# The denominator's epsilon by a one-row matmul, and the order of decode and division in the attention steps

## The chip, the cores and the metric

The kernel runs on one core of a Trainium2 chip. The metric is the device time of one execution in microseconds (us). It stood at 959.82 us, the median of three runs (958.62 to 960.18).

## The reference

A linear attention with random features, then two feed-forward layers; all inputs and outputs are fp32.

```python
q_s, k_s = (q * scale, k * scale)          # q, k, v: batch 4, 8 heads, 576 rows, head_dim 64
def phi(x):                                # omega: 128 features x 64
    proj = np.einsum('bhsd,md->bhsm', x, omega)
    sq = np.sum(x * x, axis=-1, keepdims=True) / 2.0
    h = proj - sq
    h = h - np.max(h, axis=-1, keepdims=True)
    return np.exp(h) / np.sqrt(m)
kv = np.einsum('bhsm,bhsd->bhmd', k_p, v)
z = np.sum(k_p, axis=2)
num = np.einsum('bhsm,bhmd->bhsd', q_p, kv)
den = np.einsum('bhsm,bhm->bhs', q_p, z)[..., None] + 1e-06
attn = num / den
x = attn as 2304 rows x 512
h = x @ w_in;  g = max(h, 0) + alpha * min(h, 0);  x = g @ w_out      # 512 -> 2048 -> 512
a = x @ w_a;  b = x @ w_b;  out = (a * b) @ w_out2                    # 512 -> 1536 -> 512
```

## The kernel before

**The work.** The attention is cut into 40 pieces: eight units `u` (a batch and a group of four heads) by five row tiles `t` (four of 128 rows, a last one of 64). It runs as a software pipeline of steps `s`. In one step `a_proj` (L724) projects a piece of k and an earlier piece of q into two banks `pp`; `a_max` (L738) takes row maxima `nm` from them on VectorE; `a_exp` (L747) makes `ph` by up to eight `Exp` on ScalarE; `a_kv` (L762) adds a piece to the states `kv` (the ones column in `v` also gives the sum z); `a_num` (L793) multiplies the transposed features `phT` of a q piece by the states `kvp`, into one bank `nd` of four slots of 65 columns, of which the last is the denominator; `a_t` (L779) transposes the next q piece on TensorE (`tp`) and copies it to `phT`; `a_x` (L815) transposes the divided rows `xn` (`xp`) into `xT`. `ev` (L834) gives the step of each: k and q at their step, `kv` one step after k, `t` two, `num` three and `x` four steps after q.

**The division** is in `a_num`: a `tensor_scalar` adds `EPS * M` to the four denominators read from the bank, a `reciprocal` works on the result in SBUF, and a `tensor_tensor` multiplies the 4 x 64 numerators by it. The scale of `EPS * M` is that of features left without their 1/sqrt(M).

**The steps.** The first 15 stand alone. From then on a step stands inside a step of the first feed-forward layer (class `Mlp`): `a_front` (L515) makes a 256-column `h` of 12 fp32r matmuls, ScalarE takes its two ReLU halves (`u`, `h`), VectorE joins them (`h`), ScalarE and VectorE split the result in a high and a low part (`gh`, `gl`), and in the middle of that `attn_next` (L943) puts one attention step; `a_back` (L551) makes `y`. `a_x` is put off to `A.flush()` between two such steps. `pp`, `nd`, `tp`, `xp` and `h` take turns in five PSUM banks.

**Decode.** The weights come as 64-bit words. The `Decoder` (L212) turns each piece of 128 x 512 into two fp32r parts: `bits` (L255) does four instructions on VectorE (`z`, `a`, `c`, `c`), `piece` (L283) then copies `a` to the high part `w` on ScalarE (L289) and forms the low part in two instructions, most often on GpSimd (L290, L291). It is a generator, and `D_.go(n)` (L414) takes n strides of it; three strides issue the four VectorE instructions, the fourth `w` and the low part.

**What sets the order.** Every engine works its instructions in the order in which the code issues them (`tc.manual_schedule()`); nothing reorders them. `attn_2` (L882) therefore says how decode stands against states, division and transposes:

```python
        D_.go(3)
        if s in ev["kv"]:
            a_kv(*ev["kv"][s])
        if s in ev["num"]:
            a_num(*ev["num"][s])
        D_.go()
        if s in ev["t"]:
            a_t(*ev["t"][s])
```

After the attention, the rest of the first layer and the second layer (Winograd-like products `W`, `E`, `B` and the output product `o`) follow on TensorE.

Of the kernel before, what the change touches and what calls it, by code (L numbers as in the profile page):

```python
# [9 lines left out]
F32 = mybir.dt.float32  # L10
# [3 lines left out]
ALU = mybir.AluOpType  # L14
# [4 lines left out]
P = 128  # L19
NB, NH, S, D = 4, 8, 576, 64  # L20
M = 128
# [9 lines left out]
EPS = 1e-6  # L31
# [34 lines left out]
def tile_kernel(ctx: ExitStack, tc: tile.TileContext, qT, kT, v1, omT, wbits, alpha, out):  # L66
    nc = tc.nc
# [70 lines left out]
    def pick(*ways):  # L138

        def worst(w):  # L140
            return max(load[e] + w.get(e, 0.0) for e in load)

        i = min(range(len(ways)), key=lambda i: worst(ways[i]))
        for e, x in ways[i].items():
            load[e] += x
        return i
# [63 lines left out]
    tensor, vector = Watch(nc.tensor, pe_cost), Watch(nc.vector, dve_cost)  # L210
# [239 lines left out]
    D_ = Decoder()  # L450
# [218 lines left out]
    def rpool(st, **kw):  # L669
        return st.enter_context(tc.tile_pool(side=RIGHT, **kw))  # L670

    ac = rpool(st_a, name="ac", bufs=1)
# [20 lines left out]
    def load_k(u):  # L693
        t = ld.tile([P, 2 * S], F32, tag="k", name=f"k{u}")
        if u == 0:
            nc.scalar.dma_start(out=t[:, 0:256], in_=kT[u][:, 0:256])
            nc.sync.dma_start(out=t[:, 256:], in_=kT[u][:, 256:])
        else:
            if u == 1:
                after_dve(t)  # L700
            nc.sync.dma_start(out=t, in_=kT[u])
        t_k[u] = t
# [15 lines left out]
    def slots_of(t):  # L718
        return 4 if t < 4 else 2

    def bank(name, pool=None):
        return (pool or psp[0]).tile([P, 512], F32, tag="ps", name=name)
# [39 lines left out]
    def a_kv(u, t):  # L762
        if t == 0:
            kvt[u] = pskv.tile([P, 4, D + 1], F32, tag="kv", name=f"kv{u}")
        kv = kvt[u]
        ph = phik.pop((u, t))
        for h in range(4):

            for r in (slice(0, M // 2), slice(M // 2, M)):
                tensor.matmul(kv[r, h, :], lhsT=ph[:, h if t < 4 else h % 2, r],  # L770
                                 rhs=t_v[u][:, t * VC + h * (D + 1):t * VC + (h + 1) * (D + 1)],
                                 start=(t == 0 and h == 0), stop=(t == 4 and h == 3))
        if t == 4:

            load["act"] += 0.4
            nc.scalar.activation(kvp[u % 3], kv, AF.Copy)
            kvt.pop(u)

    def a_t(u, t):  # L779

        ns = slots_of(t)
        ph = phiq.pop((u, t))
        pp = bank(f"tp{u}_{t}").rearrange("p (o m) -> p o m", m=P)
        for h in range(ns):
            tensor.transpose(pp[:, h, :], ph[:, h, :], ident)
        d = pq.tile([P, 4, P], F32, tag="phT", name=f"phT{u}_{t}", bufs=2)
        if pick({"act": 0.1 + 0.13 * ns}, {"dve": 0.1 + 0.15 * ns}):
            vector.tensor_copy(d[:, :ns], pp[:, :ns])
        else:
            nc.scalar.activation(d[:, :ns], pp[:, :ns], AF.Copy)  # L790
        phT[u, t] = d

    def a_num(u, t):  # L793


        ns = slots_of(t)
        d = phT.pop((u, t))
        kv = kvp[u % 3]
        nd = bank(f"nd{u}_{t}")[:, :4 * (D + 1)].rearrange("p (o e) -> p o e", e=D + 1)
        for h in range(ns):  # L800
            for a in range(2):
                r = slice(a * 64, a * 64 + 64)

                tensor.matmul(nd[r, h, :], lhsT=d[:, h, r], rhs=kv[:, h if t < 4 else 2 * a + h, :],
                                 start=True, stop=True)
        load["dve"] += 0.35 + 0.13 * ns
        rc = sm.tile([P, 4], F32, tag="rc", name=f"rc{u}_{t}")
        vector.tensor_scalar(out=rc[:, :ns], in0=nd[:, :ns, D], scalar1=EPS * M, scalar2=None, op0=ALU.add)
        vector.reciprocal(out=rc[:, :ns], in_=rc[:, :ns])
        xn = pq.tile([P, 4, D], F32, tag="xn", name=f"xn{u}_{t}", bufs=2)  # L810
        vector.tensor_tensor(out=xn[:, :ns], in0=nd[:, :ns, 0:D],
                                in1=rc[:, :ns].unsqueeze(2).to_broadcast([P, ns, D]), op=ALU.mult)
        xns[u, t] = xn
# [67 lines left out]

    def attn_2(s):  # L882

        D_.go(3)
        if s in ev["kv"]:
            a_kv(*ev["kv"][s])
        if s in ev["num"]:
            a_num(*ev["num"][s])
        D_.go()
        if s in ev["t"]:  # L890
            a_t(*ev["t"][s])

    def attn_3(s):
        if s in ev["x"]:
            a_x(*ev["x"][s])
# [4 lines left out]
    nc.sync.dma_start(out=om_raw, in_=omT)  # L900
    load_k(0)
    warm = ac.tile([P, P], F32, name="warm")
    vector.memset(warm, 0.0)
    make_identity(nc, ident)
    vector.tensor_scalar(out=om, in0=om_raw.rearrange("p (k n) -> p k n", n=64), scalar1=scale, scalar2=None, op0=ALU.mult)
# [8 lines left out]
    if True:  # L914
        w_ = bank("warm")
        for i in range(WARM):
            tensor.matmul(w_[:, 0:P], lhsT=warm, rhs=warm, start=True, stop=True)
        for s in range(SPLIT_AT):
            D_.step(DEC0[0] if s < 3 else DEC0[1] if s < Q_LAG else DEC0[2])
            passed(1.3 if s < Q_LAG else 4.5)  # L920
            pj = attn_1(s)
            nm = a_max(*pj)
            loads(s)

            for k in range(KT):
                if s > x_step[k // 2, (CI - 1) // P]:
                    A.split(0, 0, CI, k)
            a_exp(*pj, nm)
            if s == 3:
                D_.start(0)  # L930
            if s == Q_LAG + 1:
                nc.sync.dma_start(out=nalpha, in_=alpha)
            attn_2(s)
            attn_3(s)
        vector.tensor_scalar(out=nalpha, in0=nalpha, scalar1=-1.0, scalar2=None, op0=ALU.mult)
    st_z.close()

    with st_m:
# [4 lines left out]
        def attn_next(high=None, low=None):  # L943
            s = nxt_s[0]
            nxt_s[0] += 1
            D_.step(DEC1)
            pj = attn_1(s)
            if high:
                high()
            if pj:  # L950
                nm = a_max(*pj)
            loads(s)
            if low:
                low()
            if pj:
                a_exp(*pj, nm)
            attn_2(s)
            A.after.append(lambda: attn_3(s))
# [378 lines left out]
```

## Time and profile before

| what | value |
|---|---|
| median of the runs | 959.82 us |
| the profiled execution, own time | 958.08 us |
| its span | 956.3 us |
| TensorE (PE) busy | 937.0 us, 98% |
| TensorE weight loads (PEld) busy | 843.5 us, 88% |
| VectorE (DVE) busy | 673.4 us, 70% |
| ScalarE (ACT) busy | 515.5 us, 54% |
| GpSimd (POOL) busy | 165.0 us, 17% |
| granted TensorE clock, mean | 0.999 of full |

The profile is one execution. The shares are means over stages with different limits: attention steps fill some 235 us at the start, so the table tells little of them, and the prediction goes by stretches. A matmul's end is modelled, so a busy TensorE may still be waiting for a part of a modelled end; what is sure of a matmul is its start. An fp32 matmul shows as two records, a transpose as one.

### The profile page before, as it was taken

What the parts mean: (1) busy time and instruction counts of PE and PEld (TensorE: products, weight loads), DVE (VectorE), ACT (ScalarE), POOL (GpSimd) and SP (SyncE); (2) the same over time, 40 slices, a digit from 0 to 9 for tenths busy, and PEclk for the clock granted to TensorE, in tenths of its full rate; (3) what the DMA queues carried; (4) which work ended last, traced back from release to release, by engine and by line L of the source; (5) the groups of instructions that cost most, each with busy time, mean ns of one, the idle gap of its engine ahead of it and who ended that gap; (6) DMA issues with size and microseconds to landing.
All of it is one profiled execution on the core that took longest, in us unless ns stands there. A gap on an engine that the chain in (4) does not pass through costs nothing.

```text
span 956.3 us, 16788 instructions
## 1 busy us (share of the span) xinstructions
PE 937.0 (98%) x6486; PEld 843.5 (88%) x6486; DVE 673.4 (70%) x1343; ACT 515.5 (54%) x1237; POOL 165.0 (17%) x135
## 2 busy tenths in 40 slices
PE   7889999999999999999999999999999999999998
PEld 6778899989988878889888899999999999989897
DVE  5898855555488887768766978977686975673733
ACT  6877766655455545345544546564464554554531
POOL 3686700000056541001000000000001011110101
PEclk9999999999999999999999999999999999999999
DMA  8544422000123332304536756259828288523323
GB/s 302 171 163 148 136 77 77 26 23 24 46 88 113 108 111 88 132 22 144 202 118 219 294 213 220 77 185 372 312 86 226 58 251 273 142 34 100 43 57 66
DMA packets 47696, 132.65 MB, mean 139 GB/s; under 512 B 4352, under 2 KB 10752, under 8 KB 47616
## 3 DMA queue, kind: packets, MB, share of 16 engines
q1 hardware_dynamic: 42720, 122.79, 36.9%
q0 software_dynamic: 4752, 8.65, 6.0%
q8 instruction: 51, 0.84, 0.4%
q14 instruction: 29, 0.24, 0.1%
q10 hardware_dynamic: 144, 0.13, 0.0%
HBM read 87.52 MB, written 44.04 MB: 138 GB/s over the span
## 4 chain that ended last, share of the span: by engine, by line
PE 81%; DVE 9%; ACT 6%; issue 2%; DMA 2%; SPq 0%; DVEq 0%; ACTq 0%
PE y L188 17%; PE h L188 16%; PE o L188 15%; PE W L188 15%; PE E L188 7%; PE B L188 4%; ACT ph L757 3%; DVE a L188 2%; DVE z L188 1%; DVE c L188 1%; PE tp L188 1%; DVE h L188 1%; PE nd L188 1%; PE kv L188 1%; DMA store<-t_None 1%
## 5 line engine op out<-in xcount | busy, mean ns | idle before, releaser
L188 PE MATMUL h<-xh,w 128*128 128x256 f32 (+1 forms) x768 | 204.5, 340 | 0.2 <-DVE yo L188 0.2
L188 PE MATMUL y<-gh,w 128*128 128x256 f32 (+1 forms) x768 | 202.0, 338 | 0.9 <-ACT gh L539 0.9
L188 PEld LDWEIGHTS y<-gh,w 128*128 128x128 f32 x768 | 134.5, 189 | 16.5 <-ACT gh L539 1.6
L188 PEld LDWEIGHTS h<-xh,w 128*128 128x128 f32 x768 | 135.0, 189 | 15.8 <-DVE yo L188 0.4
L188 PE MATMUL o<-w,gh 128*128 128x512 f32 x432 | 133.2, 389 | 0.0
L188 PE MATMUL y<-gl,w 128*128 128x512 f32 (+1 forms) x384 | 129.3, 337 | 0.4 <-DVE gl L188 0.2
L188 PE MATMUL h<-xl,w 128*128 128x512 f32 (+1 forms) x384 | 129.0, 336 | 0.2 <-DVE xl L500 0.2
L188 DVE SCALAR_TENSOR_TENSOR h<-u,nalpha,h 128x256 f32<-128x256 f32 (+1 forms) x96 | 59.5, 620 | 72.9 <-ACT h L527 71.9
L526 ACT ACTIVATE u<-h 128x256 f32<-128x256 f32 (+1 forms) x96 | 47.2, 492 | 98.0 <-PE h L188 94.8
L1236 POOL DMA_DIRECT2D out<-op x30 | 26.3, 877 | 422.2 <-ACT op L163 344.2
L188 PEld LDWEIGHTS o<-w,gh 128*128 128x128 f32 x432 | 81.0, 188 | 16.5
L539 ACT ACTIVATE gh<-h 128x256 fp32r<-128x256 f32 (+1 forms) x96 | 47.1, 491 | 78.7 <-DVE h L188 78.5
L188 PE MATMUL o<-w,gl 128*128 128x512 f32 x216 | 84.2, 390 | 0.0
L290 POOL TENSOR_TENSOR a<-a,w 128x512 f32<-128x512 f32 x32 | 47.2, 1474 | 212.2 <-ACT w L289 207.2
L188 PEld LDWEIGHTS y<-gl,w 128*128 128x128 f32 x384 | 72.7, 189 | 8.7 <-DVE gl L188 1.3
L188 PEld LDWEIGHTS h<-xl,w 128*128 128x128 f32 x384 | 72.7, 189 | 7.9 <-DVE xl L500 0.5
L188 DVE TENSOR_TENSOR gl<-h,gh 128x256 fp32r<-128x256 f32 (+1 forms) x96 | 53.1, 553 | 23.6 <-ACT gh L539 22.5
L163 ACT ACTIVATE u<-W 128x384 f32<-128x384 f32 x72 | 35.0, 491 | 45.7 <-PE W L188 44.6
L188 DVE TENSOR_SCALAR z<-z 128x512 uint32<-128x512 uint32 x68 | 39.8, 585 | 24.6 <-ACT z L249 24.5
L188 DVE SCALAR_TENSOR_TENSOR a<-raw,z 128x512 uint32<-128x512 uint32 x68 | 54.0, 794 | 2.3
L163 ACT ACTIVATE op<-o 128x512 f32<-128x512 f32 x51 | 30.4, 596 | 44.4 <-PE o L188 36.6
L188 DVE SCALAR_TENSOR_TENSOR c<-raw,c 128x512 f32<-128x512 uint32 x68 | 48.5, 714 | 2.3
(492 smaller groups left out, 1987.1 us busy)
## 6 DMA issues: line engine op xcount, KB each, us to landing
raw<-in_w SPq DMA_DIRECT2D x68, 512.0 KB, 4.2
w<-store SPq DMA_DIRECT2D x39, 512.0 KB, 6.6
store<-t_None SPq DMA_DIRECT2D x34, 512.0 KB, 3.8
st<-ypart SPq DMA_DIRECT2D x14, 768.0 KB, 8.0
out<-op POOLq DMA_DIRECT2D x30, 256.0 KB, 5.2
v<-in_v SPq DMA_DIRECT2D x8, 650.0 KB, 6.0
q<-in_qT SPq DMA_DIRECT2D x8, 576.0 KB, 3.8
yp<-ypart SPq DMA_DIRECT2D x4, 1024.0 KB, 7.5
```

What stands on the lines that cost most here:

```text
L163: nc.scalar.activation(out, in_, AF.Copy)
L188: return call(*a, **k)
L290: eng.tensor_tensor(out=a, in0=a, in1=hi.bitcast(F32), op=ALU.subtract)
L526: nc.scalar.activation(u_, hp, AF.Relu, scale=-1.0)
L539: nc.scalar.activation(gh, hp, AF.Copy)
L757: nc.scalar.activation(ph[:, 2 * pr + j], pair[j][:, o + pr], AF.Exp, bias=nm[:, j, o + pr:o + pr + 1])
L1236: nc.gpsimd.dma_start(out=dst, in_=op, accum_op=ALU.add)
```

## The change

It touches three places. In `a_num`, the matmuls of a bank now form one accumulation group, which a further matmul of one row closes: 128 ones times four (or two) values `EPS * M`, added to the denominator columns in the bank. The `tensor_scalar` is gone and the `reciprocal` reads the bank. In `attn_2`, the three decode strides come after `a_kv` and `a_num`, and the fourth after `a_t`. At the start GpSimd fills the row.

```diff
@@ a_num
                 tensor.matmul(nd[r, h, :], lhsT=d[:, h, r], rhs=kv[:, h if t < 4 else 2 * a + h, :],
-                                 start=True, stop=True)
+                                 start=(h == 0), stop=False, skip_group_check=True)
         load["dve"] += 0.35 + 0.13 * ns
+        tensor.matmul(nd[:, :ns, D], lhsT=row[:, :P], rhs=row[:, P:P + ns], start=False, stop=True, skip_group_check=True)
         rc = sm.tile([P, 4], F32, tag="rc", name=f"rc{u}_{t}")
-        vector.tensor_scalar(out=rc[:, :ns], in0=nd[:, :ns, D], scalar1=EPS * M, scalar2=None, op0=ALU.add)
-        vector.reciprocal(out=rc[:, :ns], in_=rc[:, :ns])
+        vector.reciprocal(out=rc[:, :ns], in_=nd[:, :ns, D])
         xn = pq.tile([P, 4, D], F32, tag="xn", name=f"xn{u}_{t}", bufs=2)
@@ attn_2
-        D_.go(3)
         if s in ev["kv"]:
             a_kv(*ev["kv"][s])
         if s in ev["num"]:
             a_num(*ev["num"][s])
-        D_.go()
+        D_.go(3)
         if s in ev["t"]:
             a_t(*ev["t"][s])
+        D_.go()
@@ before the first step
     warm = ac.tile([P, P], F32, name="warm")
+    row = ac.tile([1, P + 4], F32, name="row")
+    nc.gpsimd.memset(row[:, :P], 1.0)
+    nc.gpsimd.memset(row[:, P:], EPS * M)
```

The order of instructions shows what moves. The three places below are of one attention step inside the first layer, the one that projects unit 4's first piece (`pp(4, 0)`); names are those of the text above, with a number behind them.

VectorE, before: from `gl` of this step to the joining `h` of the next.

```order
L188 TENSOR_TENSOR gl_256_1_1402<-h_256_1_1384,gh_256_1_1401 128x256
L188 TENSOR_SCALAR z_1344<-z_1344 128x512
L188 SCALAR_TENSOR_TENSOR a_1432<-raw_1199,z_1344 128x512
L188 TENSOR_SCALAR c_1433<-a_1432 128x512
L188 SCALAR_TENSOR_TENSOR c_1433<-raw_1199,c_1433 128x512
L188 TENSOR_SCALAR rc_1_1458<-nd_1_1449 128x4
L188 RECIPROCAL rc_1_1458<-rc_1_1458 128x4
L188 TENSOR_TENSOR xn_1_1461<-nd_1_1449,rc_1_1458 128x256
L188 SCALAR_TENSOR_TENSOR h_256_2_1477<-u_256_2_1490,nalpha,h_256_2_1477 128x256
```

The same place, now.

```order
L188 TENSOR_TENSOR gl_256_1_1405<-h_256_1_1387,gh_256_1_1404 128x256
L188 RECIPROCAL rc_1_1452<-nd_1_1442 128x4
L188 TENSOR_TENSOR xn_1_1454<-nd_1_1442,rc_1_1452 128x256
L188 TENSOR_SCALAR z_1369<-z_1369 128x512
L188 SCALAR_TENSOR_TENSOR a_1458<-raw_1220,z_1369 128x512
L188 TENSOR_SCALAR c_1459<-a_1458 128x512
L188 SCALAR_TENSOR_TENSOR c_1459<-raw_1220,c_1459 128x512
L188 SCALAR_TENSOR_TENSOR h_256_2_1480<-u_256_2_1493,nalpha,h_256_2_1480 128x256
```

The division has moved ahead of the four decode instructions and is one instruction shorter.

ScalarE, before: after the step's `Exp`, from the copy of the states to the next ReLU half.

```order
L776 ACTIVATE kvp_168<-kv_1019 128x260
L289 ACTIVATE w_88<-a_1432 128x512
L790 ACTIVATE phT_0_1471<-tp_0_1466 128x512
L831 ACTIVATE xT<-xp_0_1473 128x2x128
L526 ACTIVATE u_256_2_1490<-h_256_2_1477 128x256
```

The same place, now.

```order
L776 ACTIVATE kvp_168<-kv_1012 128x260
L790 ACTIVATE phT_0_1471<-tp_0_1466 128x512
L289 ACTIVATE w_88<-a_1458 128x512
L831 ACTIVATE xT<-xp_0_1476 128x2x128
L526 ACTIVATE u_256_2_1493<-h_256_2_1480 128x256
```

The weight copy `w` and the copy of the transposed features `phT` have changed places.

TensorE, before: from the states to the next `h`.

```order
L188 MATMUL kv_1019<-v_674,ph_4_1331 64x65 x8
L188 MATMUL nd_1_1449<-kvp_170,phT_1_1379 64x65 x8
L188 MATMUL tp_0_1466<-ident,ph_0_1190 128x128 x4
L188 MATMUL xp_0_1473<-ident,xn_0_1369 128x128 x2
L188 MATMUL h_256_2_1477<-xh_256_0_961,w_82 128x256
```

The same place, now.

```order
L188 MATMUL kv_1012<-v_677,ph_4_1334 64x65 x8
L188 MATMUL nd_1_1442<-kvp_170,phT_1_1379 64x65 x8
L188 MATMUL nd_1_1442<-row 128x4
L188 MATMUL tp_0_1466<-ident,ph_0_1193 128x128 x4
L188 MATMUL xp_0_1476<-ident,xn_0_1362 128x128 x2
L188 MATMUL h_256_2_1480<-xh_256_0_964,w_82 128x256
```

One matmul stands between the numerators and the transposes, in each of the 40 pieces; TensorE's order is otherwise the same, and so is that of the DMA queue.

## Rows read from the trace of the kernel before

**Rows 1.** Busy time by stretch; columns: stretch, length, PE, PEld, DVE, ACT, POOL, clock, DMA.
```profile
24.00:85.00 61.00, 54.31 (x730) 47.03 (x732) 54.44 (x130) 47.45 (x151) 40.34 (x29) 1.00 0.47 150
85.00:122.00 37.00, 36.23 (x451) 33.85 (x448) 29.77 (x70) 26.59 (x81) 27.53 (x19) 1.00 0.46 151
122.00:240.00 118.00, 116.67 (x1417) 108.36 (x1416) 65.81 (x193) 71.85 (x233) 0.00 (x0) 1.00 0.14 46
240.00:956.00 716.00, 710.73 (x3633) 638.12 (x3631) 509.87 (x919) 354.96 (x725) 89.17 (x77) 1.00 0.46 147
```

**Rows 2.** PE's waits from 24 to 85 us: sum, times, longest.
```profile
PE nd L188 <- ACT phT L790: 2.7, 4, 1.2
PE xp L188 <- ACT ph L757: 2.0, 3, 1.0
```

**Rows 3.** PE's waits from 85 to 240 us, all of them.
```profile
PE xp L188 <- ACT ph L757: 1.0, 2, 0.5
PE xp L188 <- DVE gl L188: 0.8, 3, 0.3
PE xp L188 <- DVE xn L188: 0.2, 1, 0.2
```

**Rows 4.** Timeline of DVE in a step: start, duration (us), instruction.
```profile
54.49 0.41 DVE L188 TENSOR_SCALAR z<-z 128x512 uint32<-128x512 uint32 x1
...
56.74 0.15 DVE L188 TENSOR_SCALAR rc<-nd 128x4 f32<-128x4 f32 x1
56.92 0.18 DVE L188 RECIPROCAL rc<-rc 128x4 f32<-128x4 f32 x1
57.14 0.42 DVE L188 TENSOR_TENSOR xn<-nd,rc 128x256 f32<-128x256 f32 x1
57.60 0.49 DVE L188 SCALAR_TENSOR_TENSOR h<-u,nalpha,h 128x256 f32<-128x256 f32 x1
```

**Rows 5.** Timeline around a wait of `nd`, ACT and PE.
```profile
23.76 0.75 ACT L289 ACTIVATE w<-a 128x512 fp32r<-128x512 f32 x1
...
24.28 0.71 ACT L790 ACTIVATE phT<-tp 128x512 f32<-128x512 f32 x1
...
25.05 0.69 PE L188 MATMUL nd<-kvp,phT 128*64 128x65 f32 x16 [1.18 <-ACT phT L790]
```

**Rows 6.** Timeline of PE, one step; a cut window shows a group's later records alone.
```profile
172.51 0.61 PE L188 MATMUL pp(7, 1)_False<-xT,q 64*128 64x128 f32 x8
...
172.74 0.39 PE L188 MATMUL pp(7, 1)_False<-xT,q 64*128 64x128 f32 x4
173.06 0.28 PE L188 MATMUL kv<-v,ph 128*64 128x65 f32 x2
...
173.16 0.58 PE L188 MATMUL kv<-v,ph 128*64 128x65 f32 x14
173.57 0.23 PE L188 MATMUL nd<-kvp,phT 128*64 128x65 f32 x2
...
173.75 0.46 PE L188 MATMUL nd<-kvp,phT 128*64 128x65 f32 x10
174.14 0.33 PE L188 MATMUL tp<-ident,ph 128*128 128x128 f32 x1
...
174.31 0.49 PE L188 MATMUL tp<-ident,ph 128*128 128x128 f32 x3
174.55 0.36 PE L188 MATMUL y<-gh,w 128*128 128x256 f32 x1
```

**Rows 7.** Records of `nd` by stretch (PE first; 16 are a piece, 8 a short one).
```profile
85.00:122.00 37.00, 3.60 (x88) 3.08 (x88) 3.33 (x12) 1.00 0.46 151
122.00:240.00 118.00, 13.24 (x312) 10.93 (x312) 11.96 (x44) 1.00 0.14 46
```

**Rows 8.** Timeline of PE and of DVE, the step with least time between `nd` and decode.
```profile
27.86 0.64 PE L188 MATMUL nd<-kvp,phT 128*64 128x65 f32 x16
...
28.72 0.42 DVE L188 TENSOR_SCALAR z<-z 128x512 uint32<-128x512 uint32 x1
```

## The prediction

> **What bounds the kernel now.** I read the busy time by stretch first, since the whole page mixes stages. Until about 85 us no engine is full: from 24 to 85 us TensorE is idle for 61.00 - 54.31 = 6.69 us and VectorE for 6.6 us [rows 1]. From 85 us on TensorE is the bound: it is idle for 0.77 us of 37 and for 1.33 us of 118 while the attention lasts, and for 5.3 us of the 716 after it, at full clock throughout [rows 1]. So time that VectorE saves can shorten the kernel only before 85 us, and time that TensorE gets to do lengthens it wherever TensorE is the bound.
>
> The waits of TensorE say what it waits for. Before 85 us the largest are for `phT`, 2.7 us in four waits, and for banks or data behind the `Exp`, 2.0 us in three [rows 2]. After it only `xp` waits, six times and 2.0 us in all [rows 3]; it waits for `xn` just once, for 0.2 us. So the divided rows are not what is late, and bringing the division ahead of decode is worth little by itself.
>
> **The change part by part.**
>
> *The add that goes.* On VectorE the `tensor_scalar` takes 0.15 us, and from its start to that of the reciprocal it is 56.92 - 56.74 = 0.18 us [rows 4]; that is what each piece saves there. How long a reciprocal takes that reads the bank is in no row. The nearest are the removed `tensor_scalar` from the same bank, 0.15 us, and the reciprocal from SBUF, 0.18 us [rows 4]; I take 0.18 us for it, and a saving of 0.18 us.
>
> *Decode behind the division.* In 15 of the 40 pieces the four decode instructions stood ahead of the division; from the `z` at 54.49 to the `tensor_scalar` at 56.74 that is 2.25 us [rows 4]. They now come later by the division, and the next `h` or `nm` on VectorE comes after both as before: the sum on the engine is the same, less the 0.18 us. Behind the wait that is added stand the four decode instructions, then the next maxima: the reciprocal must now find the bank complete at once. In the tightest step the numerators end at 27.86 + 0.64 = 28.50 us, and decode began at 28.72 [rows 8]; what the new matmul adds to the bank's completion, some 0.3 us, nearly fits. I cost the move at nothing, with 0.1 us in each of the two or three early steps if the cover is gone. The raw words are loaded in the same order.
>
> *`phT` ahead of `w`.* On ScalarE `w` at 23.76 keeps `phT` to 24.28, so 0.52 us; `nd` waits for it until 25.05, after 1.18 us of idle time [rows 5]. Where `phT` is on the path, that is won: I count it in two of the four waits [rows 2], less what the new matmul then adds to the same path of `nd`, `tp` and the next projection. `w` and the low part on GpSimd come 0.5 us later; no wait of TensorE for a weight stands in either list [rows 2, 3], so that is free.
>
> *The new matmul.* It has weights of one row by 128 columns, between `nd` of form 128\*64 and `tp` of 128\*128, so it is a form of its own. What a change of form costs is seen in one step [rows 6]. Pairs of `pp` records follow each other by (172.74 - 172.51) / 2 = 0.115 us, and pairs of `kv` records by (173.57 - 173.16) / 7 = 0.059 us. From `pp` to `kv` the last pair takes 173.06 - 172.74 - 0.115 = 0.205 us, 0.09 more than a pair, and the first `kv` pair 0.10 us, 0.04 more: 0.13 us for the change. From `nd` to `tp` it is 174.14 - 173.75 = 0.39 us for five pairs, 0.10 more than 5 x 0.059; then 0.17 us for the first transpose, against (174.55 - 174.31) / 2 = 0.12: 0.15 us. So one more change of form costs 0.13 to 0.15 us. Its two records cost as little as a `kv` pair each, 0.059 us, or as much as a `pp` pair, 0.115 us: together 0.25 to 0.38 us per piece. With no change of form at all it would be 0.12 us, and 0.06 us if the records ran side by side as those of a pair do; nothing lower, since TensorE's queue is in order and full. I take 0.30 us: the weights have the 128 columns of `pp`, but hardly any columns stream. I keep 0.06 and 0.38 us for the range.
>
> The Trainium skill (TensorEngine Tiling (Array Packing), Key Properties) has it that a change of tiling mode drains TensorE. The 0.09 and 0.10 us at the ends of `pp` and `nd` agree. The same skill (TensorE: Matmul & The Clock Gate, LDWEIGHTS) says that a load goes by its columns and not by its rows, about 107 ns for 128, so one row would save nothing; no row here has such a load alone. By that page the two loads would be an estimated 0.21 us, and the piece 0.35 us.
>
> *The sum.* After 85 us lie 88 + 312 = 400 records of `nd` [rows 7], which are 22 pieces of 16 and 6 short ones of 8: 28 pieces, 28 x 0.30 = 8.4 us on the bound engine. The six waits of `xp` hide part: each hides at most its own length or 0.30 us, so about 0.6 + 0.8 + 0.2 = 1.6 us [rows 3]. That leaves +6.8 us. Before 85 us, the path goes by VectorE and ScalarE. I count two times 0.52 us for `phT` less 0.30 us for the matmul on that path, 0.4 us; eight of the twelve pieces, in which VectorE is the path, by 0.18 us, 1.4 us; and take off two pieces in which the path has already moved to TensorE, 0.6 us, and 0.2 us for decode's lost cover. That is -1.0 us. The two fills of the row on GpSimd come before the identity is needed, some 20 us later, and cost nothing. Sum: +5.8 us. The profiled execution took 958.08 us, 1.74 us under the median; it would take 963.9 us, and I forecast 959.82 + 5.8 = **965.6 us** for the median.
>
> **The rivals.**
>
> *The matmul is cheap, and nothing changes.* If the one-row form costs no change, a piece costs 0.12 us, and 28 pieces 3.4 us, of which the waits hide 6 x 0.12 = 0.7 us; with 2.0 us won before 85 us the sum is +0.7 us: 960.5 us. For it speaks that the matmul writes four columns alone; against it, that both changes of form in the step cost time [rows 6]. The Trainium skill (TensorEngine Tiling (Array Packing), Instruction Overhead) supports the cheap case: about 60 cycles for any small matmul, by which two records are an estimated 0.05 us and 28 pieces 1.4 us; the transposes and `kv` pairs here are too long to show it.
>
> *VectorE's relief is worth all of its length, and the kernel is faster.* In the 15 pieces with decode VectorE is nearly full, so each 0.18 us may be won until 122 us, 2.7 us, and `phT` adds 2 x 0.52 = 1.0 us: 3.7 us, which the 6.69 us of idle time before 85 us [rows 1] can hold. With the matmul at 0.06 us (28 x 0.06 - 0.4 = +1.3 us) the sum is -2.4 us: 957.4 us. It decides where a piece's matmul costs less than about 0.08 us, since 22 unhidden pieces then give back no more than 1.8 us of the 3.7. Against it: from 85 to 122 us VectorE is busy for 29.77 of 37 us, so not the bound [rows 1].
>
> *The full price, and VectorE held.* At 0.38 us a piece, 28 pieces are 10.6 us, less 1.9 us hidden, with nothing won before 85 us because the reciprocal waits with decode and maxima behind it: +8.7 us, 968.5 us. This is the upper part of my range. That the change does not do what it says, a reciprocal from the bank as long as the 0.33 us of both instructions before, would take 1.4 us from the gain, and is inside the range too.
>
> **How the numbers follow.** A difference within 0.2%, 1.9 us, is about what a measurement of this kernel cannot tell from no change. The forecast, slower by 2 to 10 us, with the full price at its upper end, gets 0.70; the cheap matmul without a gain 0.15; the faster case 0.15. So faster 0.15, same 0.15, slower 0.70. The range goes from 958.0 us, inside the cheap case, to 969.5 us, a little over the full price; what is left out is most of the faster case and a rest above, under 0.2 together.
>
> **What would show it.** Right: in steps after 85 us the distance from `nd`'s first record to `tp`'s grows from 0.57 us by 0.25 to 0.38 us, with the new records in between; TensorE has no new idle time there; the step at the end of the attention comes some 6 us later than before; the 716 us after it keep their length. On VectorE the reciprocal follows `gl` without idle time, at 0.15 to 0.25 us; at 85 us the kernel stands 0 to 3 us ahead. Wrong: if that distance grows by less than 0.13 us, the price of the form failed; if it grows by 0.3 us and the kernel still isn't slower, TensorE was not the bound where I say so; if VectorE waits ahead of the reciprocal, the cover of the move was gone.

## The result, and the profile after

The changed kernel takes **967.98 us**, the median of five runs (966.15 to 968.65); before stood at 959.82 us in five runs beside them. The ratio is 1.0082, with an interval of 1.0072 to 1.0093: 8 us slower. Forecast were 965.6 us in a range of 958.0 to 969.5.

The profiled execution took 968.65 us, with a span of 966.9 us; it is the slowest of the five, while the profiled one of before was among the fastest of its kernel, so that the two traces differ by 10.57 us, 2.4 more than the medians. Part of this spread goes with the clock, in both kernels alike: after takes 966.15 us at a mean granted clock of 1.000 and 968.65 at 0.995 and 0.996, and of 61 executions of before that ran beside the experiments the 13 at 1.000 have a median of 958.19 us and the 24 at 0.997 or less one of 959.88.

The busy time of after by stretch, with the columns of [rows 1]:

```profile
24.00:85.00 61.00, 55.68 (x748) 49.38 (x746) 53.24 (x115) 46.40 (x150) 38.65 (x27) 0.97 0.47 150
85.00:122.00 37.00, 36.44 (x461) 33.87 (x460) 30.69 (x67) 27.35 (x83) 26.86 (x20) 1.00 0.45 153
122.00:240.00 118.00, 117.80 (x1416) 110.14 (x1415) 59.20 (x161) 69.29 (x224) 2.28 (x2) 1.00 0.13 42
240.00:956.00 716.00, 712.62 (x3669) 641.46 (x3668) 511.61 (x927) 358.59 (x735) 88.34 (x76) 1.00 0.46 146
```

From 85 us on TensorE was nearly full before and is fuller now: 117.80 of 118 us, where it was 116.67. New in this table is the 0.97 in the clock's column of the first row: in the changed kernel the clock was not full all the time ahead of 85 us; in [rows 1] it is 1.00 there.

TensorE's waits in after, from 24 to 85 us (two rows) and, behind the dots, from 85 to 240 us (one row, all there is); they answer to [rows 2, 3]:

```profile
PE xp L188 <- ACT ph L757: 2.3, 3, 1.5
PE nd L188 <- ACT phT L790: 1.8, 3, 0.7
...
PE xp L188 <- ACT ph L757: 0.8, 2, 0.6
```

`nd` waits less for `phT` (1.8 us, was 2.7), `xp` a little more before 85 us, and of the 2.0 us of waits behind 85 us 0.8 are left.

One step of TensorE in after, the same as in [rows 6]:

```profile
177.67 0.64 PE L188 MATMUL nd<-kvp,phT 128*64 128x65 f32 x16
178.23 0.38 PE L188 MATMUL nd<-row 1*128 1x4 f32 x2
178.54 0.66 PE L188 MATMUL tp<-ident,ph 128*128 128x128 f32 x4
```

The new matmul is two records. From the first `nd` to the first `tp` it is 178.54 - 177.67 = 0.87 us, where [rows 6] have 174.14 - 173.57 = 0.57; from the 7th piece on, every piece with a `tp` behind it takes 0.30 or 0.31 us more than before. In VectorE's timeline of the same step the reciprocal reads the bank and takes 0.17 us, with no idle time ahead of it. It waits for the bank in one piece alone, the first (last row):

```profile
178.51 0.42 DVE L188 TENSOR_TENSOR gl<-h,gh 128x256 fp32r<-128x256 f32 x1
178.84 0.17 DVE L188 RECIPROCAL rc<-nd 128x4 f32<-128x4 f32 x1
179.05 0.43 DVE L188 TENSOR_TENSOR xn<-nd,rc 128x256 f32<-128x256 f32 x1
...
26.22 0.18 DVE L188 RECIPROCAL rc<-nd 128x4 f32<-128x4 f32 x1 [0.29 <-PE nd L188]
```

Where the time of the two profiled executions parts is read from the starts of three pieces' numerators, the 1st, the 13th and the last, on TensorE. (The start of the 1st says little by itself: over the fourteen traces of this study it lies anywhere from 24.1 to 27.6 us.) Before (the 1st is in [rows 5]):

```profile
85.30 0.64 PE L188 MATMUL nd<-kvp,phT 128*64 128x65 f32 x16
...
234.15 0.45 PE L188 MATMUL nd<-kvp,phT 128*64 128x65 f32 x8
```

After:

```profile
25.18 0.69 PE L188 MATMUL nd<-kvp,phT 128*64 128x65 f32 x16 [0.67 <-ACT phT L790]
...
86.81 0.64 PE L188 MATMUL nd<-kvp,phT 128*64 128x65 f32 x16
...
241.56 0.45 PE L188 MATMUL nd<-kvp,phT 128*64 128x65 f32 x8
```

| stretch | before, us | after, us | difference |
|---|---|---|---|
| to the 1st piece | 25.05 | 25.18 | +0.1 |
| 1st to 13th | 60.25 | 61.63 | +1.4 |
| 13th to 40th | 148.85 | 154.75 | +5.9 |
| 40th to the end of the span | 722.15 | 725.34 | +3.2 |

The last row is not the change's: `nd` is done by then. It comes from one place near 745 us, where ScalarE waits for a store to land (first row) and TensorE behind it (second row); the last two rows show the 4 us that follow, with the columns of [rows 1].

```profile
745.41 0.42 ACT L163 ACTIVATE t<-a 128x256 fp32r<-128x256 f32 x1 [6.58 <-DMA store<-t_None]
...
746.26 0.44 PE L188 MATMUL W<-xh11A,w 128*128 128x384 f32 x1 [2.23 <-ACT u L163]
...
747.00:749.00 2.00, 2.00 (x9) 2.00 (x8) 1.93 (x5) 1.07 (x3) 0.00 (x0) 0.53 0.01 4
749.00:751.00 2.00, 2.00 (x9) 2.00 (x8) 2.00 (x5) 0.00 (x0) 0.00 (x0) 0.62 0.86 238
```

TensorE waits 2.23 us for `W`, 0.7 in before, and then runs 4 us at a clock of 0.53 and 0.62. In the profiled execution of the first experiment, which has the new matmul too, the same stretch takes 722.2 us (962.7 - 240.53), as in before; of the twelve experiments' traces eleven have 721.4 to 723.3 us there, with a new matmul or without, and one 725.7. So the differences that belong to the change are +1.4 us, where a gain of 1.0 was forecast, and +5.9, where 6.8 were.

### The profile page after: what moved, and what is told of

Its sections match the earlier page's. It is cut to its first block, busy times and chain, and to the rows that moved or that the text cites. A ratio compares the mean times of both kernels' runs of the same rounds, so it can differ in the third digit from the quotient of the medians.

```text
span 966.9 us, 16931 instructions
## 1 busy us (share of the span) xinstructions
PE 948.3 (98%) x6566; PEld 856.3 (89%) x6566; DVE 669.6 (69%) x1303; ACT 515.7 (53%) x1237; POOL 165.2 (17%) x137
## 4 chain that ended last, share of the span: by engine, by line
PE 82%; DVE 8%; ACT 5%; issue 2%; DMA 2%; SPq 0%; DVEq 0%; ACTq 0%
PE y L188 16%; PE h L188 16%; PE W L188 15%; PE o L188 15%; PE E L188 7%; PE B L188 4%; ACT ph L757 2%; PE nd L188 2%; DVE a L188 2%; DVE z L188 2%; PE tp L188 1%; PE kv L188 1%; DVE c L188 1%; DMA store<-t_None 1%; DVE h L188 1%
```

## The experiments

Two questions stood: is the new matmul the whole loss, and by what, its change of form or its records; and what did the new order do before 85 us? At first the theory was the prediction's price of the form; the rivals were the records alone, and the order. Ratios are to before, run on the same chip beside the kernels that are compared with it; its median was 959.92 us in 19 runs, 959.24 in 29 and 959.35 in 13. Where a kernel ran once, no ratio is given.

### The two halves of the change apart

The first kernel keeps the new matmul and the reciprocal from the bank, and puts `attn_2` back:

```diff
+        D_.go(3)
         if s in ev["kv"]:
...
             a_num(*ev["num"][s])
-        D_.go(3)
+        D_.go()
         if s in ev["t"]:
             a_t(*ev["t"][s])
-        D_.go()
```

> The changed kernel with decode put back ahead of states and division; the one-row matmul and the reciprocal from the bank stay. Theory A (the matmul's price on a full TensorE): nd to tp stays 0.31 us longer, and the time stays 6 to 8 us over the kernel before, 966 to 968 us. Theory B (the moved order: weight copies, GpSimd and VectorE late, TensorE idle and then at the lower clock): at most half of the loss is left, 963 us or less.

Measured: 965.81 us in four runs (964.08 to 968.13), ratio 1.0070 (1.0046 to 1.0094). From the 1st to the 13th piece it takes 85.47 - 24.94 = 60.53 us, from there to the last 240.53 - 85.47 = 155.06, 6.2 us more than before.

The second is the kernel before with the new `attn_2` alone:

```diff
-        D_.go(3)
         if s in ev["kv"]:
...
             a_num(*ev["num"][s])
-        D_.go()
+        D_.go(3)
         if s in ev["t"]:
             a_t(*ev["t"][s])
+        D_.go()
```

> The kernel before with the new order alone; add and reciprocal stay two VectorE instructions. Theory A: within 1.5 us of the kernel before, 958.5 to 961.5 us, since decode's sum on VectorE is unchanged. Theory B: at least half of the loss, 963 us or more, with TensorE idle near 49 us and a stretch at the lower clock behind it.

Measured: 961.11 us in ten runs (958.67 to 962.58), ratio 1.0017 (1.0006 to 1.0028). From the 1st to the 13th piece 87.66 - 25.39 = 62.27 us, 2.0 more than before; from there to the last 148.68, 0.2 less. The time is in the range of theory A; the trace, below, has the idle TensorE and the lower clock of theory B.

So the matmul costs 0.70% or 6.7 us, by the trace nearly all of it behind 85 us; the new order costs 0.17% or 1.6 us, by the trace ahead of 85 us. Together that is 8.3 us, and the whole change cost 8.2. That they add up so well is partly luck: by the intervals the matmul costs 4.4 to 9.0 us and the order 0.6 to 2.7. The order, of which a gain was forecast, is a loss.

### What the matmul costs by: form, records, width

Four variants of the added matmul, all with the change's order, and all adding the same epsilon. The first has the form of `nd`: 128 rows of weights, 64 columns, two of them side by side.

```diff
-    row = ac.tile([1, P + 4], F32, name="row")
-    nc.gpsimd.memset(row[:, :P], 1.0)
+    row = ac.tile([P, P + 4], F32, name="row")
+    nc.gpsimd.memset(row[:, :P], 1.0 / P)
...
-        tensor.matmul(nd[:, :ns, D], lhsT=row[:, :P], rhs=row[:, P:P + ns], start=False, stop=True, skip_group_check=True)
+        for r in (slice(0, 64), slice(64, 128)):
+            tensor.matmul(nd[r, :ns, D], lhsT=row[:, :64], rhs=row[:, P:P + ns], start=False, stop=True, skip_group_check=True)
```

> The changed kernel, its epsilon added by two matmuls of 128 rows and 64 columns (rows of 1/128), the form of the numerators, so that no other form stands between numerators and transposes. If the price is that of the form, four records follow at the pairs' 0.054 us, nd to tp grows by 0.11 us instead of 0.31, and the time is 961 to 964 us. If it is that of two more fp32 matmuls whatever their form, nd to tp grows by 0.3 us or more and the time stays at 966 us or above.

Measured: 960.97 us in ten runs (959.03 to 963.40), ratio 1.0015 (1.0003 to 1.0027): what the order alone costs. So the matmul in this form, together with the VectorE add that it saves, costs nothing that these times can show. The trace shows a little of each: 1.3 us more than the order alone from the 13th piece to the last (149.94 against 148.68), 0.8 us less from the 1st to the 13th (61.46 against 62.27). The accumulation group is the changed kernel's here too, so it is not what costs. One step on TensorE:

```profile
176.97 0.64 PE L188 MATMUL nd<-kvp,phT 128*64 128x65 f32 x16
177.44 0.23 PE L188 MATMUL nd<-row 128*64 128x4 f32 x4
177.60 0.66 PE L188 MATMUL tp<-ident,ph 128*128 128x128 f32 x4
```

The second issues the change's one-row matmul twice, with half of epsilon each:

```diff
-    nc.gpsimd.memset(row[:, P:], EPS * M)
+    nc.gpsimd.memset(row[:, P:], EPS * M / 2)
...
+        tensor.matmul(nd[:, :ns, D], lhsT=row[:, :P], rhs=row[:, P:P + ns], start=False, stop=False, skip_group_check=True)
         tensor.matmul(nd[:, :ns, D], lhsT=row[:, :P], rhs=row[:, P:P + ns], start=False, stop=True, skip_group_check=True)
```

> The changed kernel with the one-row matmul given twice, half of epsilon each: two more records and no further change of form. If the form is the price, nd to tp grows by another 0.05 to 0.12 us. If the records are (0.13 us from the first to the second in the changed kernel), it grows by 0.27 us more.

Measured, in one run: 972.3 us. One step:

```profile
181.57 0.64 PE L188 MATMUL nd<-kvp,phT 128*64 128x65 f32 x16
182.13 0.60 PE L188 MATMUL nd<-row 1*128 1x4 f32 x4
182.67 0.65 PE L188 MATMUL tp<-ident,ph 128*128 128x128 f32 x4
```

The third has 128 rows and 128 columns, so the form that `tp` has behind it: the tile of the first variant with the change's own matmul, `lhsT=row[:, :P]`.

```diff
-    row = ac.tile([1, P + 4], F32, name="row")
-    nc.gpsimd.memset(row[:, :P], 1.0)
+    row = ac.tile([P, P + 4], F32, name="row")
+    nc.gpsimd.memset(row[:, :P], 1.0 / P)
```

> The changed kernel, its epsilon added by one matmul of 128 rows (1/128 each) and 128 columns, the form of the transposes that follow: the two records and their weights stay, the further change of form goes. If a change of form is worth 0.09 us and the two records 0.22 (as two more records cost in the run with two one-row matmuls), nd to tp grows by 0.21 to 0.24 us over the kernel before, and the time is 964 to 966 us. If the form is most of the price, it grows by 0.17 us or less, below 964 us. If form is nothing, 0.31 us stay.

Measured: 964.82 us in four runs (962.45 to 967.03), ratio 1.0062 (1.0038 to 1.0086). One step:

```profile
179.01 0.64 PE L188 MATMUL nd<-kvp,phT 128*64 128x65 f32 x16
179.58 0.39 PE L188 MATMUL nd<-row 128*128 128x4 f32 x2
179.83 0.63 PE L188 MATMUL tp<-ident,ph 128*128 128x128 f32 x4
```

The fourth has one row, and the two 64-column halves of the first variant:

```diff
-        tensor.matmul(nd[:, :ns, D], lhsT=row[:, :P], rhs=row[:, P:P + ns], start=False, stop=True, skip_group_check=True)
+        for r in (slice(0, 64), slice(64, 128)):
+            tensor.matmul(nd[r, :ns, D], lhsT=row[:, :64], rhs=row[:, P:P + ns], start=False, stop=True, skip_group_check=True)
```

> The changed kernel, its epsilon added by two matmuls of one row and 64 columns each: the further change of form stays, the weights are half as wide and stand in two column halves. If wide weights are the larger part, nd to tp grows by 0.12 to 0.22 us; if the change of form is, by 0.25 us or more.

Measured, in one run: 963.47 us. One step:

```profile
176.62 0.64 PE L188 MATMUL nd<-kvp,phT 128*64 128x65 f32 x16
177.19 0.28 PE L188 MATMUL nd<-row 1*64 1x4 f32 x4
177.40 0.66 PE L188 MATMUL tp<-ident,ph 128*128 128x128 f32 x4
```

From the first `nd` to the first `tp`, by these rows, against the 0.57 us of before:

| added matmul | form | records | `nd` to `tp`, us | more than before |
|---|---|---|---|---|
| as changed | 1\*128 | 2 | 0.87 | 0.30 |
| twice | 1\*128 | 4 | 1.10 | 0.53 |
| full form | 128\*128 | 2 | 0.82 | 0.25 |
| one row, halves | 1\*64 | 4 | 0.78 | 0.21 |
| `nd`'s form, halves | 128\*64 | 4 | 0.63 | 0.06 |

Two further records of 128 columns add 0.23 us, so 0.115 each, the distance that the prediction had read off the `pp` pairs. The full form pays 0.25 us for two of them, with no more changes of form than before had, and the one-row form 0.05 more. A change of form where the records are cheap costs more: the halves of one row cost 0.15 us more than the same halves in `nd`'s form. So the parts do not add up: a change of form costs 0.15 us next to narrow weights and 0.05 next to wide ones. (In both pairs the number of rows changes together with the form; no run tells the two apart.) With 128-column weights the records are most of the price. That `nd`'s form is cheap needs both, the halves and no change of form.

### What the order costs by

The traces of the order alone and of after are alike ahead of 85 us, with the same kinds of waits and 62.27 and 61.63 us from the 1st to the 13th piece. VectorE in after, and behind the dots GpSimd, in the first step that stands inside the feed-forward layer:

```profile
44.85 0.69 DVE L188 SCALAR_TENSOR_TENSOR a<-raw,z 128x512 uint32<-128x512 uint32 x1
...
46.65 1.24 DVE L188 TENSOR_SCALAR nalpha<-nalpha 128x16 f32<-128x16 f32 x1
48.01 0.49 DVE L188 SCALAR_TENSOR_TENSOR h<-u,nalpha,h 128x256 f32<-128x256 f32 x1
...
46.29 1.57 POOL L290 TENSOR_TENSOR a<-a,w 128x512 f32<-128x512 f32 x1 [2.88 <-ACT w L289]
```

The same place before:

```profile
44.09 0.69 DVE L188 SCALAR_TENSOR_TENSOR a<-raw,z 128x512 uint32<-128x512 uint32 x1
...
46.63 0.50 DVE L188 TENSOR_SCALAR nalpha<-nalpha 128x16 f32<-128x16 f32 x1
47.25 0.49 DVE L188 SCALAR_TENSOR_TENSOR h<-u,nalpha,h 128x256 f32<-128x256 f32 x1
...
45.53 1.56 POOL L290 TENSOR_TENSOR a<-a,w 128x512 f32<-128x512 f32 x1 [2.98 <-ACT w L289]
```

The decode instruction `a` is 0.76 us later than before, `w` follows it on ScalarE, and so the subtraction on GpSimd starts at 46.29 instead of 45.53. In this step VectorE negates the 16 columns of `nalpha`, once in the kernel. That ends with GpSimd's subtraction in both traces: 46.63 + 0.50 = 47.13 against 45.53 + 1.56 = 47.09 before, 46.65 + 1.24 = 47.89 against 46.29 + 1.57 = 47.86 after. In all fourteen traces it ends 0.03 us after a subtraction of GpSimd's, and takes from 0.27 to 1.25 us until then. The join `h` behind it starts 0.76 us later; behind the join come the row maxima on VectorE, and behind these the `Exp` that `xp` on TensorE waits for, 1.50 us instead of 1.02:

```profile
49.93 0.44 PE L188 MATMUL xp<-ident,xn 128*128 128x128 f32 x2 [1.50 <-ACT ph L757]
```

Then the clock falls. TensorE in after, by 2 us:

```profile
48.00:50.00 2.00, 0.50 (x5) 0.27 (x4) 1.95 (x6) 1.39 (x5) 2.00 (x2) 1.00 0.93 267
50.00:52.00 2.00, 2.00 (x13) 2.00 (x14) 1.90 (x5) 2.00 (x7) 0.96 (x1) 0.70 0.70 237
52.00:54.00 2.00, 2.00 (x17) 1.77 (x17) 1.71 (x3) 1.17 (x4) 1.90 (x2) 0.50 0.34 72
```

In the two stretches after the idle one it is granted 0.70 and 0.50; 0.50 is the lower level, 1.2 GHz. In before TensorE is busy for 0.97 us of 48 to 50 us, and the clock is 1.00 in all three stretches. The kernel with the order alone does as after does, with a longer wait of `xp` (2.23 us):

```profile
46.94 1.24 DVE L188 TENSOR_SCALAR nalpha<-nalpha 128x16 f32<-128x16 f32 x1
...
50.00:52.00 2.00, 1.78 (x9) 1.78 (x10) 1.88 (x6) 1.70 (x6) 0.98 (x1) 0.58 0.44 172
52.00:54.00 2.00, 2.00 (x15) 1.77 (x16) 1.72 (x3) 1.85 (x5) 1.27 (x1) 0.57 0.00 0
```

The new theory (C in the expectations) was that this meeting of `nalpha` with the subtraction makes the loss. It is tried by negating `nalpha` some steps earlier, in the changed kernel, in the order alone and in before:

```diff
+            if s == Q_LAG + 3:
+                vector.tensor_scalar(out=nalpha, in0=nalpha, scalar1=-1.0, scalar2=None, op0=ALU.mult)
             if s == Q_LAG + 1:
...
-        vector.tensor_scalar(out=nalpha, in0=nalpha, scalar1=-1.0, scalar2=None, op0=ALU.mult)
```

> The changed kernel with one small VectorE instruction, the negation of nalpha, issued six steps earlier, away from GpSimd's subtraction behind the later weight copy. Theory C (that instruction is held until the subtraction ends, and the idle TensorE then falls to the lower clock): the join of the first h comes some 0.7 us earlier, xp waits less than 1.2 us near 49 us, no stretch at the lower clock near 51 us, and the time falls by 1.5 to 2.5 us, to 965.5 to 966.5 us. Theory D (the moved order itself leaves TensorE idle there): the lower clock stays, and the time with it.

> The new order alone, with nalpha negated early. Theory C: the 1.2 us that the order alone cost are gone, 958.0 to 960.0 us, and no lower clock near 50 us. Theory D: as the order alone, 961 us.

> The kernel before with nalpha negated early. Theory C: the instruction was held for 0.5 us there too, so xp waits 0.4 us less near 49 us and the time is 959.0 to 959.9 us, hardly to be told from the kernel before. Theory D: no change.

Measured: the changed kernel 966.63 us in six runs, ratio 1.0068 (1.0052 to 1.0084), against 1.0082 without; the order alone 959.88 us in twelve, 1.0008 (0.9998 to 1.0017), against 1.0017; before 959.46 us in twelve, 1.0002 (0.9994 to 1.0011). By the ratios the first two lose 1.3 and 0.9 us of what they cost, in the direction of the theory, but the intervals overlap. The traces tell why it is not more: in the changed kernel the join starts at 46.35 us, the wait at 48.27 is down to 0.54 us, and the clock is 1.00 there; but the next `xp` then waits 1.39 us at 54.61. In its step VectorE's `xl` takes 1.34 us, 0.69 in before, beside GpSimd's subtraction of 50.64 us. In the order alone the low clock stands at 56 to 60 us instead. So `nalpha` is one of several meetings; moving it moves the wait.

The lower clock is not what the loss consists of. Two traces with the new order keep the full clock from 24 to 85 us, that of the changed kernel with early `nalpha` (first row) and that of the matmul in its full form (second row), in which `xp` waits longer than in after (third row):

```profile
24.00:85.00 61.00, 55.51 (x750) 48.88 (x752) 54.00 (x116) 47.01 (x151) 39.26 (x28) 1.00 0.47 148
...
24.00:85.00 61.00, 53.75 (x761) 47.35 (x762) 53.62 (x113) 46.87 (x151) 38.97 (x28) 1.00 0.46 150
...
52.29 0.44 PE L188 MATMUL xp<-ident,xn 128*128 128x128 f32 x2 [1.68 <-ACT ph L757]
```

From the 1st to the 13th piece they take 61.31 and 61.35 us, where after takes 61.63 and before 60.25. So of the 1.4 us that after loses there, some 0.3 may go with the clock, and 1.1 are lost without it.

The order has two parts, decode behind the division, and `phT` ahead of `w`. Each alone, in the kernel before; first `phT` ahead of `w`, with decode where it was:

```diff
             a_num(*ev["num"][s])
-        D_.go()
         if s in ev["t"]:
             a_t(*ev["t"][s])
+        D_.go()
```

> The kernel before with the copy of the transposed features ahead of the weight copy alone; decode's four VectorE instructions stay first, and nalpha is negated where it was. If it is the later weight copy that makes GpSimd's subtraction late and holds nalpha, nalpha takes about 1 us or more near 46 us and the time is 960 to 962 us, over the same kernel with nalpha early (958.5 us). If the loss came from decode standing behind the division, nalpha takes 0.5 us and the time is 957.5 to 959.5 us.

Measured: 958.67 us in ten runs (957.77 to 959.67), ratio 0.9995 (0.9985 to 1.0005). Then decode behind the division, with `w` ahead of `phT`:

```diff
-        D_.go(3)
         if s in ev["kv"]:
             a_kv(*ev["kv"][s])
         if s in ev["num"]:
             a_num(*ev["num"][s])
+        D_.go(3)
         D_.go()
```

> The kernel before with decode's four VectorE instructions behind states and division, and the weight copy ahead of the transposed features as before. The weight copy then waits for decode and holds phT behind it on ScalarE: nd waits 0.5 us or more longer in the early steps and the time is 961 to 964 us. If the weight copy finds decode done anyway, the time is within 1 us of the kernel before.

Measured: 963.63 us in four runs (963.29 to 964.17), ratio 1.0050 (1.0035 to 1.0066). So the loss is that of decode's move, 0.50% by itself. The traces say the same: all nine with decode behind the division take 61.3 to 63.0 us from the 1st piece to the 13th, all five without it 59.8 to 60.5. That `w` waits for the later `a` and keeps `phT` behind it, as expected, is seen in full in one step (two rows); the third row is a later wait of `xp`:

```profile
39.46 0.63 ACT L289 ACTIVATE w<-a 128x512 fp32r<-128x512 f32 x1 [0.78 <-DVE a L188]
...
40.63 0.69 PE L188 MATMUL nd<-kvp,phT 128*64 128x65 f32 x16 [0.85 <-ACT phT L790]
...
69.42 0.60 PE L188 MATMUL xp<-ident,xn 128*128 128x128 f32 x2 [1.72 <-DVE xn L188]
```

But the time of that wait is made up by the next piece, and `nd`'s waits for `phT` grow from 2.7 to 3.1 us only. What grows more is the waits of `xp`: 5.7 us from 24 to 88 us, 2.5 in before and 4.9 with the order alone. `phT` ahead of `w` gives back 0.33%, some 3 us, of this loss; of that the traces show plainly only the first wait of `nd`, 1.18 us without it and 0.66 with it. By itself `phT` ahead of `w` is worth nothing that can be told from zero.

`phT` ahead of `w` together with the early `nalpha`, in the kernel before (the two diffs on `nalpha` and on `phT` above), was run as a version that might beat both kernels:

> The kernel before with the copy of the transposed features ahead of the weight copy alone (decode's four VectorE instructions stay ahead of states and division), and nalpha negated early. The wait of nd for phT near 25 us shrinks by 0.5 us, and with theory C nothing is paid for it: 958.0 to 959.5 us, the fastest of all. If phT is not on the path, it is the same as nalpha negated early alone.

Measured: 958.46 us in twelve runs (957.14 to 960.33), ratio 0.9992 (0.9983 to 1.0001). It is the fastest median of the study, and not clearly faster than before. `nd`'s form of the matmul together with that order was not run.

## Why the prediction was right in its range, and where not

- **The bound.** Right: behind 85 us what TensorE gets to do is paid. TensorE's idle time there fell from 0.77 + 1.33 = 2.10 us to 0.56 + 0.20 = 0.76.
- **The price of a piece, 0.30 us.** Right in sum: 0.30 in the step shown, 0.30 or 0.31 from the 7th piece on. Its composition was off. The prediction put 0.13 to 0.15 us to the change of form and 0.12 to 0.23 to two records; with weights of 128 columns two records cost 0.23 and the form 0.05. It took 0.30 as a middle value, in which a form too dear and records too cheap cancel; that the sum fits so well is luck. The rule of the Trainium skill (TensorE: Matmul & The Clock Gate, LDWEIGHTS), that a load goes by its columns and one row saves nothing, agrees: 0.115 us per further record, and the full form of 128 rows is not dearer than one row. The cheap rival, and the rule of the Trainium skill (TensorEngine Tiling (Array Packing), Instruction Overhead) beside it, do not: 0.23 us for two further small matmul records, where by that rule they would be an estimated 0.05.
- **How much the waits hide.** From the 13th to the 40th piece lie 27 prices of 0.30 us, 8.1 us; 5.9 us were paid, 6.2 with the matmul alone. So 1.9 to 2.2 us were hidden, 1.6 forecast; 1.3 of it is the idle time that went. The rest does not show as idle time; it may lie in the ends of matmuls, which are modelled, but no trace shows it.
- **The gain of 1.0 us ahead of 85 us.** Wrong, and in sign: 1.4 us were lost there in the profiled execution. Three terms made it. "Decode behind the division ... I cost the move at nothing" failed: it costs 0.50% by itself. The prediction looked for its price at the reciprocal, which waits once, 0.29 us at the first piece, where 0.2 us were put down for it; in the step read above it fell on what stands behind decode's `a`, which is `w`, then GpSimd's subtraction, then VectorE beside it. "`w` and the low part on GpSimd come 0.5 us later ... so that is free" failed for the same reason: TensorE waits for no weight, as said, but for what comes by way of VectorE. The 1.4 us for eight pieces of VectorE's relief, less 0.6 for two pieces of the matmul on the path, did not come either: the instruction is gone and 0.18 us a piece with it, but the matmul alone, which holds both, takes 60.53 us from the 1st to the 13th piece, where before took 60.25. No run has the relief by itself. Under the new order some of it shows: the order alone takes 62.27 us there, after and the three variants of 0.06 to 0.25 us a piece 61.35 to 61.63. The sign that was given for this term failed with it: at the 13th piece the kernel stands 86.81 - 85.30 = 1.5 us behind, not 0 to 3 ahead. Only `phT` did as said: `nd`'s wait in [rows 5] fell from 1.18 to 0.67 us, and the sum of [rows 2] from 2.7 to 1.8; but as a part of the whole it is not measurable.
- **The sum.** +6.7 us for the matmul and +1.6 for the order make the 8.2, within their intervals; forecast were +6.8 and -1.0. So the first term held, and the 2.4 us by which the number came out low are those of the second. The rival of the full price with VectorE held, 968.5 us, is nearest in number, and yet not what happened: a piece costs 0.30 us, not 0.38, and the reciprocal waits 0.29 us in all.
- **What stays open.** That VectorE is held by GpSimd's subtraction is read from equal ends in each trace and from `nalpha`'s early move, which changed the time less than its interval; a kernel that has the low parts elsewhere was not tried. That the later waits of `xp` come by the same way as the first is argued, not shown. Why the clock fell after a wait of 1.50 us in after is open too: it kept its level after the 1.68 us of the full form above, and with `phT` ahead of `w` alone TensorE also waits 1.50 us there, and keeps the clock:

```profile
49.45 0.44 PE L188 MATMUL xp<-ident,xn 128*128 128x128 f32 x2 [1.50 <-ACT ph L757]
...
50.00:52.00 2.00, 2.00 (x24) 1.87 (x24) 1.86 (x6) 1.97 (x6) 0.68 (x2) 1.00 0.41 160
```

## What to carry to other kernels

A matmul that is added to a full TensorE to spare VectorE an instruction paid here by its weights' columns and by its change of form; that it had one row and four streamed columns made it no cheaper. In the form of its neighbours, in halves, it cost 0.06 us a piece, against 0.30, and with the VectorE add that it spared nothing that the times can show. Whoever moves work later on one engine has to follow its results through the other engines to the first instruction that is on the path, not only to the nearest wait: here the division came earlier, hardly anything waited for it, and what was moved behind it went, in the step read above, by ScalarE and GpSimd into a join that TensorE does wait for. A forecast can stay in its range while one of its terms has the wrong sign; the parts, run apart, show it.

## What was not expected of the hardware

- A VectorE instruction on 16 columns took 0.50 us in before, 0.69 in the first experiment and 1.24 in after, each time until a GpSimd subtraction ended; in all fourteen traces the two ends lie 0.03 us apart. The Trainium skill (GPSIMD Engine Reference, Specifications) names interfaces to SBUF that GpSimd shares with VectorE, with contention for a VectorE instruction in a 2-port mode or with two inputs from SBUF; the equal ends agree, and no trace shows the mode.
- A wait of TensorE of 1.5 to 2.2 us was followed by 2 to 4 us at a granted clock near 0.5 to 0.7, three times above; after waits of 1.50 and 1.68 us in two other kernels the clock stayed full. Near 745 us, where TensorE was full, the wait was 1.5 us longer than in before and the stretch 3.2 us, so a wait may cost more than its length; ahead of 85 us, where TensorE was not, the lower clock made some 0.3 us at most, by the traces.
- The same change of form, with that of the rows, cost 0.15 us next to 64-column weights and 0.05 next to 128-column ones.
